# Attention and MLP on one core: five value buffers, later query transfers, a later LayerNorm subtraction, and turns of seven heads at the end

## The chip, the cores and the metric

The kernel runs on one NeuronCore of a Trainium2 chip. TensorE (PE in the profile; PEld are its weight loads) multiplies, ScalarE (ACT) does exponentials, GELU and copies, VectorE (DVE) does maxima, subtractions and the last scaling, GpSimd (POOL) does element-wise work in on-chip memory, and SyncE (SP) issues transfers. ScalarE and GpSimd issue transfers too. Products land in PSUM, eight banks of 128 x 512 float32. The metric is the device time of one execution in microseconds (us); three runs of the kernel before are shown.

## The reference

```python
g = sigmoid((x * gate_w).sum(-1, keepdims=True))
a = attention(x, wqkv, wo)      # 16 heads of 28, no mask, softmax over 2048 keys
b = gelu(layernorm(x) @ w1 + b1) @ w2 + b2
return g * a + (1 - g) * b      # x: (1, 2048, 448), all float32; MLP width 1792
```

LayerNorm has no weights (eps 1e-5), GELU is the tanh form.

## The kernel before

Every float32 operand is split into a high part that the fast float32 product takes exactly and a low rest; a product is high x high + high x low + low x high. A contraction runs over 32 rows at a time: the 128 rows of the array make four *strips*, and four instructions on different strips run side by side.

**First stage: a planner.** The class `Strips` writes the order of the TensorE instructions by simulating the four strips with costs and due times of its own. Its pieces of work are `QK` (queries and keys), `Val` (values and the gate's sum), `Up` and `Down` (the two MLP products), each over one bank of banks 0 to 5, each visited by all four strips in some order. When one strip is done with a piece and the next may add to the same bank, SyncE passes the word on (line 529, `hand`; three times for each of 113 pieces, 339 in all): so a transfer that SyncE has to issue, or has to wait for, stands in the same queue as these hand-offs. `st.at(t, fn)` puts `fn` into the program where the planner's clock reaches `t`; the engines keep that order.

Between the pieces the planner puts *row maxima* (`RowMax`): a product of 128 queries with 512 keys into bank 6 or 7 (line 212), and VectorE's maximum of it (line 214). There are 1024, counted by strip and by chunk n (four heads x 512 queries, 16 chunks); softmax needs them before the exponentials. When a strip has ended chunk n, the queries of chunk n + 2 are fetched into the same half of `qd` (`load_q`, line 196), set by line 511 at the planner's time plus 1.5.

`Val.close` (line 322) has ScalarE copy a finished bank into `vt[i % 3]` and send it to memory (`vs<-vt`, line 328). LayerNorm of x goes by chunks c of 512 tokens (`want_ln`): x is loaded, the mean subtracted (VectorE for c of 0 and 1, line 683; GpSimd after that, line 679), multiplied by 1/std (line 688), split into `yh` (ScalarE, line 704) and `yl` (GpSimd, line 705), which `Up` reads.

**Second stage: turns.** The attention proper has 1024 *heads* (a strip's key block of 128 against 512 queries). `turn_of` takes five or six of them: two halves of at most three. For each half PE makes three passes (line 1152: high x high, low x high, high x low), each head on its strip and in its bank, then ScalarE takes the exponentials of the half's banks in one instruction (line 1156) into `p0` or `p1`, three buffers each. `turn_bank` puts head i of a turn in bank (i + shift) % 6, shift being 0 or 3 as the first stage ended. Row maxima still owed are put between the passes (`lone`), in bank 6 or a free one: three in a turn of five, two in a turn of six. A turn has five heads only while more is owed than the turns up to the last 116 heads could take.

After a turn's scores come value products (`batch`, line 1164: four heads at once, into bank 7), of earlier turns' exponentials. In a turn of six `quota` allows one and a half batches, or two if more than two are behind; in other turns all that are there. When a chunk's 16 batches are done, `valued` has VectorE copy bank 7 into `ob`, fetch the sums, and GpSimd multiply (`finish_a`, `finish_b`, `finish_c`; the last chunk's `finish_last` does this and the projection in one go). In the last group of heads four *projections* follow, in turns 6 to 9 after the chunk (`tail`, `project`, lines 1001 to 1009: twelve products into bank 6, the weighted sum, the output).

Pool `ao` gives two buffers each to `ob`, `rc` and `lt` and six to `acc`; the raw output weights (`fetch_wo`) use `ob`.

Of the kernel before, what the change touches and what calls it, by code (L numbers as in the profile page):

```python
# [15 lines left out]
P = 128  # L16
S = 2048
D = 448
# [17 lines left out]
def kernel(ctx: ExitStack, tc: tile.TileContext, xt, wqk, wv, wo, xk, w1, b1, w2, b2,  # L36
# [84 lines left out]
    mr = px.tile([P, 2, NT], F32, name="mr")  # L121
    mrt = px.tile([P, 2 * NT], F32, name="mrt")
    std = px.tile([P, NT], F32, name="std")
    vt = [px.tile([P, H, 32], F32, name=f"vt{i}") for i in range(3)]

    bxr = [px.tile([P, 2, D], F32, name=f"bxr{i}") for i in range(2)]

# [173 lines left out]
    class Val(Piece):  # L301
# [18 lines left out]
            return ops  # L320

        def close(self, st, now):
            v, ps, tt = vt[self.i % 3], bk[:, self.bank], self.i
            nc.scalar.activation(v[:, :, 0:DH], ps[:, :D].rearrange("p (h d) -> p h d", d=DH), AF.Copy)
            nc.scalar.activation(zall[:, tt:tt + 1], ps[:, D:D + 1], AF.Copy)
            st.use("act", now + 0.2, 0.75)
            st.free[self.bank] = st.act + 0.1
            st.at(st.act + 0.3, lambda: nc.scalar.dma_start(vs[tt], v.rearrange("p (g j) d -> p g (j d)", g=NG)), act=0.35)
# [75 lines left out]
    class Strips:  # L404
# [92 lines left out]
        def rowmax(self, s, now):  # L497
            if now < self.hot[s] or not rowmax.ready(s):
                return False
            if rowmax.cnt[s] > 5 + min(rowmax.cnt):  # L500
                return False
            b = min(self.rm, key=lambda b: self.rm[b])
            if self.rm[b] > now:
                return False
            ends = rowmax.one(s, bk[:, b])
            self.t[s] = now + 0.232
            self.use("dve", now + 0.45, RM)
            self.rm[b] = self.dve + 0.1
            for kind, n, j in ends:
                if kind == "q":  # L510
                    self.at(now + 1.5, lambda n=n, j=j: rowmax.load_q(n, j))
                elif kind == "k":
                    def load(n=n, j=j):
                        rowmax.load_k(n, j)
                        self.hot[j] = self.get(self.clock + 0.6, 224) + 1.0

                    self.at(now + 1.5, load)
                    self.hot[j] = 1e9
                else:
                    self.at(now + 0.5, lambda n=n: rowmax.close(n), dve=0.45)  # L520
                    self.at(now + 3.0, lambda n=n: rowmax.store(n))
            return True
# [151 lines left out]
    def want_ln(st, c):  # L674
        cs = slice(c * CH, (c + 1) * CH)

        def use(t, r):
            if c > 1:
                nc.gpsimd.tensor_sub(r, r, lnr[c][:, 0])
                st.use("pool", st.clock, 1.35)  # L680
                scale(t, r)
                return
            nc.vector.tensor_sub(r, r, lnr[c][:, 0])
# [13 lines left out]
        st.feed.pump()  # L697
# [267 lines left out]
    wraw = {}  # L965

    def fetch_wo(g):
        wraw[g] = ao.tile([P, D], F32, name="ob")
        nc.sync.dma_start(wraw[g], wo[:, g])

    def split_wo(g):
# [45 lines left out]
    obs = {}  # L1017

    def finish_a(n):
        ob = ao.tile([P, CH], F32, name="ob")  # L1020
        lt = ao.tile([P, CH // 32], F32, name="lt")
        obs[n] = ob, lt
        nc.vector.tensor_copy(ob, pv)  # L1023
# [1 line left out]

    def finish_b(n):
        ob, lt = obs[n]
        rc = ao.tile([P, CH], F32, name="rc")
        obs[n] = ob, rc
        nc.vector.reciprocal(lt, lt)  # L1030
        r = rls[n]
# [13 lines left out]
    def finish_last(n):  # L1045

        g, c = divmod(n, NC)
        ob = ao.tile([P, CH], F32, name="ob")
        rc = ao.tile([P, CH], F32, name="rc")
# [78 lines left out]
    def turn_of(u, turn):  # L1128

        left = UNITS - u  # L1130
        owed = rowmax.left()
        size = min(left, 5 if owed and owed > 2 * ((left - 116) // 6) else 6)
        na, nb = min(3, size), max(0, size - 3)
        for x in range(u, u + size):
            n = x // 64
            if n not in begins:
                begins.add(n)
                begun(n, turn)
        extra = {5: ((0, 3, 6), (3, 1, 5), (5, 2, 6)), 6: ((0, 3, 6), (5, 2, 6))}.get(size, ())
        for half, first, count in ((0, 0, na), (1, 3, nb)):  # L1140
            for p in range(3):
                for x, o, b in extra:
                    if x == 3 * half + p:
# [1 line left out]
                for i in range(first, first + count):  # L1145
# [6 lines left out]
                    nc.tensor.matmul(bk[:, turn_bank(i)], w[r, ks], q[r], start=(p == 0), stop=(p == 2), skip_group_check=True)  # L1152
            if count:
                t = ap.tile([P, 3, CH], F32, name=f"p{half}")
                b = turn_bank(first)
                nc.scalar.activation(t[:, :count], bk[:, b:b + count], AF.Exp, scale=SCALE)  # L1156
                for i in range(count):
                    prob[u + first + i] = t[:, i]
# [14 lines left out]
    while b < UNITS // 4:  # L1173
        before, quota = u, 99
        if u < UNITS:
            u += turn_of(u, turn)
            if u - before == 6:
                quota = 3 + (before // 4 - b > 2)
        for fn in agenda.pop(turn, ()):
            fn()  # L1180
# [72 lines left out]
```

## Time and profile before

| what | value |
| --- | --- |
| runs | 1093.5, 1094.56, 1097.05 us; median 1094.56 |
| the profiled execution | 1093.69 us, its span 1091.9 us |
| mean granted TensorE clock | 0.996 |
| PE busy / PEld busy | 1074.4 us (98%) / 728.4 us (67%) |
| DVE / ACT / POOL busy | 740.4 / 634.0 / 368.7 us |
| row maxima before 455 us / after | 566 / 458 |
| last row maximum's product | 984.6 us |
| instructions | 30966 |

The first stage ends at about 455 us, when the first score products (line 1152) run. PE's busy time says little by itself: up to four strips overlap, and the record counts a moment as busy if any of them works. A wait shows as PE idle time only when all four strips have run dry. The waits name what came last; the chain that ended last tells where such a wait lay on the way to the end. All times are in us from the span's start unless they are marked ns.

### The profile page before, as it was taken

What the parts mean: (1) busy time and instruction counts of PE and PEld (TensorE: products, weight loads), DVE (VectorE), ACT (ScalarE), POOL (GpSimd) and SP (SyncE); (2) the same over time, 40 slices, a digit from 0 to 9 for tenths busy, and PEclk for the clock granted to TensorE, in tenths of its full rate; (3) what the DMA queues carried; (4) which work ended last, traced back from release to release, by engine and by line L of the source; (5) the groups of instructions that cost most, each with busy time, mean ns of one, the idle gap of its engine ahead of it and who ended that gap; (6) DMA issues with size and microseconds to landing.
All of it is one profiled execution on the core that took longest, in us unless ns stands there. A gap on an engine that the chain in (4) does not pass through costs nothing.

```text
span 1091.9 us, 30966 instructions
## 1 busy us (share of the span) xinstructions
PE 1074.4 (98%) x13394; PEld 728.4 (67%) x13394; DVE 740.4 (68%) x1186; ACT 634.0 (58%) x660; POOL 368.7 (34%) x384
## 2 busy tenths in 40 slices
PE   9999999999999999999999999999999999999998
PEld 7999998999899899844444444444444444454655
DVE  4899898898999999866776665667676544311102
ACT  5343363033043132287788788788787888857572
POOL 4565587336234037341001101310110313445431
PEclk9999999999999999999999999999999999999999
DMA  7696433212100104320000001300000201011111
GB/s 248 201 293 196 153 110 93 78 43 71 45 2 11 45 3 126 93 74 16 29 6 23 23 21 48 88 28 8 21 25 19 80 21 55 20 57 38 61 53 60
DMA packets 47785, 73.20 MB, mean 67 GB/s; under 512 B 13840, under 2 KB 28816, under 8 KB 46848
## 3 DMA queue, kind: packets, MB, share of 16 engines
q1 hardware_dynamic: 33888, 39.11, 11.8%
q0 software_dynamic: 5120, 16.89, 5.3%
q10 hardware_dynamic: 8640, 15.21, 3.9%
q8 instruction: 105, 1.72, 0.6%
q14 instruction: 32, 0.26, 0.1%
HBM read 51.75 MB, written 19.31 MB: 65 GB/s over the span
## 4 chain that ended last, share of the span: by engine, by line
PE 95%; ACT 1%; DMA 1%; DVE 1%; issue 1%; SPq 0%; DVEq 0%; ACTq 0%
PE bk L488 34%; PE bk L1164 22%; PE bk L1152 19%; PE bk L212 15%; PE bk L1001 1%; PE bk L1002 1%; PE bk L1003 1%; ACT p L1156 1%; PE bk L917 1%; DMA vs<-vt 1%; DMA gbs<-gb 1%; PE bk L902 0%; DVE ob L1023 0%; PE bk L945 0%; DVE acc L1008 0%
## 5 line engine op out<-in xcount | busy, mean ns | idle before, releaser
L214 DVE TENSOR_REDUCE mx<-bk 128x1 f32<-128x512 f32 x1024 | 674.2, 688 | 219.5 <-PE bk L212 188.4
L1156 ACT ACTIVATE p<-bk 128x1536 f32<-128x1536 f32 (+1 forms) x387 | 481.8, 1298 | 135.4 <-PE bk L1152 129.4
L212 PE MATMUL bk<-kd,qd 28*128 28x512 f32 x1024 | 449.2, 441 | 2.8 <-DVE acc L1008 1.7
L212 PEld LDWEIGHTS bk<-kd,qd 28*128 28x128 f32 x1024 | 186.4, 182 | 186.6 <-DVE mx L214 117.2
L488 PE MATMUL bk<-yh,w1f 32*128 32x512 f32 x1568 | 188.6, 393 | 2.5 <-ACT gb L398 2.5
L488 PE MATMUL bk<-yl,w1f 32*128 32x512 f32 x784 | 164.2, 393 | 0.0
L488 PEld LDWEIGHTS bk<-yh,w1f 32*128 32x128 f32 x1568 | 151.1, 183 | 5.7 <-ACT gb L398 3.7
L488 PE MATMUL bk<-w2h,hh 32*128 32x448 f32 x896 | 140.6, 368 | 2.2 <-SPq L529 2.2
L488 PE MATMUL bk<-w2l,hh 32*128 32x448 f32 x896 | 140.0, 366 | 0.0
L1164 PE MATMUL bk<-p,va 128*32 128x512 f32 (+1 forms) x1080 | 130.6, 579 | 0.0
L1164 PE MATMUL bk<-p,vb 128*32 128x512 f32 (+1 forms) x1192 | 129.4, 540 | 0.0
L363 POOL TENSOR_TENSOR hl<-h,hh 128x512 fp32r<-128x512 f32 x56 | 72.3, 1301 | 140.5 <-ACT hh L356 79.3
L837 POOL CAST yh<-yl 128x512 fp32r<-128x512 f32 x16 | 9.8, 614 | 285.7 <-PE bk L212 89.7
L1152 PE MATMUL bk<-yh,ka 29*128 29x512 f32 x512 | 104.3, 481 | 0.6 <-ACT p L1156 0.6
L488 PEld LDWEIGHTS bk<-w2h,hh 32*128 32x128 f32 x896 | 102.2, 185 | 3.3 <-SPq L529 2.6
L488 PEld LDWEIGHTS bk<-yl,w1f 32*128 32x128 f32 x784 | 103.3, 184 | 0.3
L488 PEld LDWEIGHTS bk<-w2l,hh 32*128 32x128 f32 x896 | 102.3, 185 | 0.1
L1152 PE MATMUL bk<-yh,kb 29*128 29x512 f32 x512 | 96.8, 478 | 0.7 <-ACT p L1156 0.5
L398 ACT ACTIVATE gb<-bk 128x448 f32<-128x448 f32 x14 | 7.6, 545 | 140.1 <-PE bk L488 98.8
L488 PE MATMUL bk<-w2h,hl 32*128 32x448 f32 x896 | 88.0, 362 | 0.0
L1152 PE MATMUL bk<-yh,la 28*128 28x512 f32 x512 | 86.3, 392 | 0.0
L1152 PE MATMUL bk<-yl,ka 28*128 28x512 f32 x512 | 84.7, 410 | 0.0
(141 smaller groups left out, 1603.5 us busy)
## 6 DMA issues: line engine op xcount, KB each, us to landing
qk<-qo ACTq DMA_DIRECT2D x28, 256.0 KB
raw<-in_xt SPq DMA_DIRECT2D x17, 256.0 KB
vs<-vt ACTq DMA_DIRECT2D x16, 256.0 KB
rc<-rls SPq DMA_DIRECT2D x60, 64.0 KB
bxr<-in_xk POOLq DMA_DIRECT2D x8, 448.0 KB, 6.1
acc<-gbs SPq DMA_DIRECT2D x16, 224.0 KB
out_y<-acc SPq DMA_DIRECT2D x16, 224.0 KB
qd<-qk SPq DMA_DIRECT2D x60, 56.0 KB
```

The costliest lines, as they stand in the source:

```text
L212: nc.tensor.matmul(ps, self.qd[n % 2][r, i * P:(i + 1) * P], self.kd[r, k * 512:(k + 1) * 512], start=True, stop=True)
L214: nc.vector.reduce_max(self.mx[n % 2][:, j, i, k:k + 1], ps, axis=AX)
L363: nc.gpsimd.tensor_sub(hl[f], h, hh[f].bitcast(F32))
L488: mm = nc.tensor.matmul(bk[:, x.bank, :n], a, b, start=x.first, stop=(len(x.rem) == 1 and m == len(ops) - 1), skip_group_check=True)
L837: nc.gpsimd.tensor_copy(h, l.bitcast(F32))
L917: nc.tensor.matmul(bk[:, b], w, v, start=(i == 0), stop=(i == len(ops) - 1), skip_group_check=True)
L1001: nc.tensor.matmul(po, h, woh[:, g], start=(g == 0), stop=False, skip_group_check=True)
L1002: nc.tensor.matmul(po, h, wol[:, g], start=False, stop=False, skip_group_check=True)
L1003: nc.tensor.matmul(po, l, woh[:, g], start=False, stop=(g == NG - 1), skip_group_check=True)
L1152: nc.tensor.matmul(bk[:, turn_bank(i)], w[r, ks], q[r], start=(p == 0), stop=(p == 2), skip_group_check=True)
L1156: nc.scalar.activation(t[:, :count], bk[:, b:b + count], AF.Exp, scale=SCALE)
L1164: nc.tensor.matmul(bk[32 * j:32 * j + 32, 7, sl], vg[n // NC][:, k, 32 * j:32 * j + 32], prob[4 * b + j][:, sl], start=(k == 0), stop=(k = ...
```

## The change

Five edits. `vt` has five buffers in place of three. `load_q` in the first stage is put at the planner's time plus 6.0 in place of 1.5. For chunk 0 of LayerNorm VectorE's subtraction is put 1.5 of the planner's time after its load is expected. The raw output weights use buffers of `acc`, and `ob` and `rc` have one buffer each. And a turn that begins with no row maximum owed takes seven heads, unless a projection is due in it or in the next turn: four heads in banks 0 to 3, three in banks 4 to 6; `p0` gets room for four.

```diff
-    vt = [px.tile([P, H, 32], F32, name=f"vt{i}") for i in range(3)]
+    vt = [px.tile([P, H, 32], F32, name=f"vt{i}") for i in range(5)]
...
-            v, ps, tt = vt[self.i % 3], bk[:, self.bank], self.i
+            v, ps, tt = vt[self.i % 5], bk[:, self.bank], self.i
...
-                    self.at(now + 1.5, lambda n=n, j=j: rowmax.load_q(n, j))
+                    self.at(now + 6.0, lambda n=n, j=j: rowmax.load_q(n, j))
...
-        def use(t, r):
+        def use(t, r, late=False):
             if c > 1:
                 nc.gpsimd.tensor_sub(r, r, lnr[c][:, 0])
                 st.use("pool", st.clock, 1.35)
                 scale(t, r)
+                return
+            if c == 0 and not late:
+                st.at(st.clock + 1.5, lambda: use(t, r, True))
                 return
             nc.vector.tensor_sub(r, r, lnr[c][:, 0])
...
-        wraw[g] = ao.tile([P, D], F32, name="ob")
+        wraw[g] = ao.tile([P, D], F32, name="acc", bufs=6)
...
-        ob = ao.tile([P, CH], F32, name="ob")
+        ob = ao.tile([P, CH], F32, name="ob", bufs=1)
...
-        rc = ao.tile([P, CH], F32, name="rc")
+        rc = ao.tile([P, CH], F32, name="rc", bufs=1)
...
-        size = min(left, 5 if owed and owed > 2 * ((left - 116) // 6) else 6)
-        na, nb = min(3, size), max(0, size - 3)
+        size = 5 if owed and owed > 2 * ((left - 116) // 6) else 6
+        if not owed and not (tail and tail[0][0] <= turn + 1):
+            size = 7
+        size = min(left, size)
+        na = min(4 if size == 7 else 3, size)
+        nb = size - na
...
-        for half, first, count in ((0, 0, na), (1, 3, nb)):
+        place = (lambda i: i) if size == 7 else turn_bank
+        for half, first, count in ((0, 0, na), (1, na, nb)):
...
-                    nc.tensor.matmul(bk[:, turn_bank(i)], w[r, ks], q[r], ...)
+                    nc.tensor.matmul(bk[:, place(i)], w[r, ks], q[r], ...)
             if count:
-                t = ap.tile([P, 3, CH], F32, name=f"p{half}")
-                b = turn_bank(first)
+                t = ap.tile([P, 4 - half, CH], F32, name=f"p{half}")
+                b = place(first)
...
-            if u - before == 6:
+            if u - before > 5:
                 quota = 3 + (before // 4 - b > 2)
```

More of the change, by code (lines that the diff above doesn't have):

```diff
@@ L1047, in finish_last @@
         g, c = divmod(n, NC)
-        ob = ao.tile([P, CH], F32, name="ob")
-        rc = ao.tile([P, CH], F32, name="rc")
+        ob = ao.tile([P, CH], F32, name="ob", bufs=1)
+        rc = ao.tile([P, CH], F32, name="rc", bufs=1)
         lt = ao.tile([P, CH // 32], F32, name="lt")
@@ L1151, in turn_of @@
                     q = (qh, qh, ql)[p][n % 3]
-                    nc.tensor.matmul(bk[:, turn_bank(i)], w[r, ks], q[r], start=(p == 0), stop=(p == 2), skip_group_check=True)
+                    nc.tensor.matmul(bk[:, place(i)], w[r, ks], q[r], start=(p == 0), stop=(p == 2), skip_group_check=True)
             if count:
-                t = ap.tile([P, 3, CH], F32, name=f"p{half}")
-                b = turn_bank(first)
+                t = ap.tile([P, 4 - half, CH], F32, name=f"p{half}")
+                b = place(first)
                 nc.scalar.activation(t[:, :count], bk[:, b:b + count], AF.Exp, scale=SCALE)
```

## The prediction

> **What bounds the kernel now.** I read the page first, its busy times and the chain that ended last.
>
> ```profile
> PE 1074.4 (98%) x13394; PEld 728.4 (67%) x13394; DVE 740.4 (68%) x1186; ACT 634.0 (58%) x660; POOL 368.7 (34%) x384
> PE 95%; ACT 1%; DMA 1%; DVE 1%; issue 1%; SPq 0%; DVEq 0%; ACTq 0%
> ```
>
> TensorE carries 95% of the chain, so an edit pays only where it shortens PE's own work or takes away a moment in which all strips stand still. Such moments are few. I looked for them in the list of waits, then in the chain around 100 us, then in busy times by short stretches (columns: stretch, length, PE, PEld, DVE, ACT, POOL busy, granted clock, DMA share, GB/s).
>
> ```profile
> PE bk L488 <- SPq L529: 2.2, 1, 2.2
> PE bk L488 <- ACT zall L325: 1.9, 1, 1.9
> ACT vt L324 <- DMA vs<-vt: 8.8, 2, 6.8
> ```
> ```profile
> 101.41 7.29 DMA vs<-vt
> 109.43 0.47 PE bk L488
> ```
> ```profile
> 110.00:114.00 4.00, 4.00 (x52) 4.00 (x50) 3.31 (x6) 0.00 (x0) 1.27 (x1) 0.60 0.37 139
> 192.00:196.00 4.00, 4.00 (x52) 3.96 (x56) 2.12 (x4) 0.00 (x0) 1.24 (x1) 0.61 0.78 257
> 296.00:300.00 4.00, 2.96 (x49) 2.67 (x52) 2.66 (x5) 1.09 (x2) 0.00 (x0) 1.00 0.44 162
> ```
>
> The two longest stops of PE in the first stage are 1.9 us (behind ScalarE, itself 6.8 us behind a value transfer) and 2.2 us (behind a hand-off on SyncE). After each the granted clock is 0.60 over four us, so 4 x 0.4 = 1.6 us of work are lost on top. The stop of 1.0 us at 296 (PE busy 2.96 of 4.00) left it at 1.00. The changed turns lie behind 985 us.
>
> **The change part by part.**
>
> *Five value buffers.*
>
> ```profile
> 92.41 0.33 ACTq L328 DMA_DIRECT2D vs<-vt  x1
> 98.40 0.33 ACTq L328 DMA_DIRECT2D vs<-vt  x1
> 100.04 0.55 ACT L324 ACTIVATE vt<-bk 128x448 f32<-128x448 f32 x1 [1.61 <-PE bk L488]
> 108.77 0.54 ACT L324 ACTIVATE vt<-bk 128x448 f32<-128x448 f32 x1 [6.83 <-DMA vs<-vt]
> ```
>
> The sixth copy waits for the third buffer, sent at 98.40 and landed at 108.7. With five buffers it takes the first, sent at 92.41 and free by 100.04, where the fourth copy waited for PE alone. The third buffer is then wanted two pieces later, after 108.7. The wait goes, and with it 1.9 us of stop and 1.6 us of slow clock: -3.5 us. Bounds: -3.5, and 0 if something else is late at that place (a rival).
>
> ```profile
> L874 POOL MEMSET vt<- 128x48 f32 x3 | 0.4, 139 | 0.0
> ```
>
> Four more small memsets on GpSimd at the start stand ahead of any data: nothing; uncovered, four of at most 139 ns would cost 0.6 us.
>
> The Trainium skill ("TensorE: Matmul & The Clock Gate", section "Why this matters for your kernels") says that idle gaps of PE up to about 3 us do not throttle it. By that rule the buffers would be worth 1.9 us alone and the sum below would be -1.5 us. The trace disagrees: a stop of 1.9 us was followed by a clock of 0.60.
>
> *Later query transfers.* SyncE's queue around the other stop:
>
> ```profile
> 184.56 0.34 SPq L196 DMA_DIRECT2D qd<-qk  x1
> 187.96 2.58 SPq L569 DMA_DIRECT2D raw<-in_xt  x4
> 190.65 0.98 SPq L196 DMA_DIRECT2D qd<-qk  x1
> ```
>
> Four loads of 2.58 us and one query load stand between two hand-offs; PE waits for the second. Moved by 4.5 us, the load at 190.65 leaves this place, but the one at 184.56 comes to 189.1, into the same burst. So I take 0. Bounds: -2.6 us (the 0.98 us of its issue, and the 1.6 us of clock, since a stop of 1.0 keeps it), and +1.0 us, one load more in the burst. The queries themselves are not late: their next use is a whole chunk, 64 maxima, later. Behind a waiting `load_q` on SyncE stand hand-offs, and PE behind these; key loads now pass the query loads, which are four short issues.
>
> *Later subtraction.* VectorE is the in-order engine here; row maxima queue behind it, and through banks 6 and 7 PE.
>
> ```profile
> L571 POOL DMA_DIRECT2D raw<-in_xt x4: 539/539/557, 100.2 to 101.8; - x4
> DMA to landing us min/median/max: 6.8/8.0/9.5
> ```
> ```profile
> 110.59 0.68 DVE L683 TENSOR_TENSOR raw<-raw,lnr 128x512 f32<-128x512 f32 x1
> 124.75 1.29 POOL L705 TENSOR_TENSOR yl<-raw,yh 128x512 fp32r<-128x512 f32 x1 [1.26 <-ACT yh L704]
> 126.86 0.49 PE L488 MATMUL bk<-yh,w1f 32*128 32x512 f32 x2
> ```
>
> The four loads land between 107 and 111. The first subtraction ran at 110.59, held up by the very stop that goes; 3.5 us earlier it would stand at 107.1 and wait for its load. At 1.5 us later it stands at 108.6, behind the first landing. It cannot gain against the kernel before, where no idle time stands ahead of line 683; it keeps the first edit's gain: 0, and as the upper bound the first rival below.
>
> *Buffers of the second stage.* `ob` and `rc` single: the copy of chunk n waits for GpSimd's use of chunk n - 1, set four turns after that chunk, and a chunk is nine turns or more. Five turns of 3 us cover it: 0. Without cover bank 7 would be held. The weights in `acc` take SyncE's waits for two `ob` buffers away; nobody on the path waited for them: 0.
>
> *Turns of seven.* From ScalarE's rows behind 985 us (duration min/median/max; and start, duration of a run of instructions):
>
> ```profile
> L1156 ACT ACTIVATE p<-bk x43: 1024/1451/1468, 985.8 to 1072.5; 128x1536 f32<-128x1536 f32 x42, 128x1024 f32<-128x1024 f32 x1
> ```
> ```profile
> 985.79 2.79 ACT L1156 ACTIVATE p<-bk 128x1536 f32<-128x1536 f32 x2 [3.92 <-PE bk L1152]
> 988.78 5.48 ACT L1156 ACTIVATE p<-bk 128x1536 f32<-128x1536 f32 x4 [0.20 <-PE bk L1152]
> 1005.20 2.79 ACT L1156 ACTIVATE p<-bk 128x1536 f32<-128x1536 f32 x2 [0.24 <-PE bk L1152]
> 1072.51 1.02 ACT L1156 ACTIVATE p<-bk 128x1024 f32<-128x1024 f32 x1 [2.87 <-PE bk L1152]
> ```
>
> 42 x 3 + 2 = 128 heads, six of them in the turn at 985.79, which holds the last row maximum: 122 heads remain. Before, these are 20 turns of six and one of two; eight carry a projection. Following the new rule by hand (chunk 13 ends in the first of them, chunk 14 ten turns later): five turns of seven, five of six, five of seven, three of six, one of four. That is two turns fewer; the last projection of chunk 14 falls behind the last chunk's own.
>
> What a turn costs, from the chain:
>
> ```profile
> 999.29 1.86 PE bk L1164 x24
> 1001.15 1.60 PE bk L1152 x13
> 1002.75 1.43 PE bk L1164 x16
> 1004.18 1.80 PE bk L1152 x13
> 1061.77 1.43 PE bk L1164 x16
> 1065.83 1.59 PE bk L1152 x16
> ```
> ```profile
> 1004.11 0.19 PEld L1152 LDWEIGHTS bk<-yh,kb 29*128 29x128 f32 x3 [0.84 <-ACT p L1156]
> 1005.01 0.19 PEld L1152 LDWEIGHTS bk<-yh,kb 29*128 29x128 f32 x3 [0.36 <-ACT p L1156]
> ```
>
> Scores take 1.60 us, values 1.43 for one and a half batches and 1.86 for two (0.86 a batch and 0.14), a projection 1065.83 - 1061.77 - 1.43 = 2.63. Seven heads are six passes as six are, the fourth strip being free: 1.60 too. The turn at 1004.11 took 1.80, since its second half began at 1005.01, when the exponentials of the previous second half had ended (1002.16 + 2.79 = 4.95 less 1000): 0.20 late.
>
> Without waits: two turns less 2 x (1.60 + 0.14) = -3.5, the last turn of four in place of two +0.4, one projection less ahead of the end -2.6: -5.7. Behind the end the late projection adds:
>
> ```profile
> 1086.57 0.22 PE bk L1003
> 1087.94 0.59 DVE acc L1008
> ```
>
> PE is free at 1086.8; twelve products at about 0.21 (the row of the last one is 0.22) end by 1089.4, and VectorE's 0.59 behind them at 1090.1, where now it ends at 1088.5: +1.6.
>
> ```profile
> L1156 ACT ACTIVATE p<-bk 128x1536 f32<-128x1536 f32 x250 | 356.3, 1451 | 132.5 <-PE bk L1152 126.5 <-PE bk L212 5.9
> L1156 ACT ACTIVATE p<-bk 128x1024 f32<-128x1024 f32 x137 | 139.6, 1019 | 2.9 <-PE bk L1152 2.9
> ```
>
> The waits grow. A four-bank exponential is not in the trace; 1019 ns for two banks and 1451 for three give 1.88 for four. With 1.45 for the second and 0.11 of overlap (5.48 for four of 1.45) a turn's exponentials end 1.09 + 3.22 = 4.31 after its scores began, against 3.88 now. I carried this row by row through the turns: each half starts when its strip is free and its banks' exponentials ended 0.06 ago. For the kernel before it gives 83.8 us from 988.78 to 1072.51, measured 83.7, of them 2.1 us of waits. For the sevens it gives 6.6: besides the second halves there is a change of banks at each change of kind. Into the first seven, banks 0 to 3 hold the previous second half's (0.9); out of a seven into a six whose first half has banks 3 to 5, it waits again (0.5 and 1.35). By the plan of the kernel before the sixes start at bank 3; started at 0 the waits are 5.4. So +4.5, or +3.3.
>
> Tail: -5.7 + 1.6 + 4.5 = +0.4 us, with the other bank order -0.8; bounds -4.1 (no new waits) and +7.3 (a rival).
>
> **Sum.** -3.5 + 0 + 0 + 0.4 = -3.1 on the profiled execution's 1093.69: 1090.6. The runs' median is 0.9 above that execution; I take half of that on top, 1091.0. A run or two of this kernel can tell about 0.3%, 3.3 us; the forecast lies at that edge.
>
> **The rivals.**
>
> *The gain is handed back by LayerNorm.* `yl` ended at 126.04 and PE began `Up` at 126.86. PE comes 3.5 us sooner; if the late subtraction keeps the chain of loads, VectorE and GpSimd where it was, PE stops 2.7 us there and the clock falls again (1.6). Against it: the chain now also loses ScalarE's second wait for a value buffer (the rest of the 8.8). Then 1091.0 + 4.3 = 1095.3.
>
> *More goes than I count.* The stop at 189 shrinks (-2.6), and the bank order is the better one (-1.2): 1091 - 3.8 = 1087.2. For it: both follow the new plan, whose order I cannot see.
>
> *ScalarE holds every seven.* If a seven's first scores wait for the whole previous turn, it takes 4.38 us in place of 3.69 on the average of my rows: ten times, 6.9 us, 1097.9. It makes the change slower by over 0.3% (1097.8) from 0.68 us a turn on. Against it: the turn at 1004.11 began while exponentials ran to 1004.95. The Trainium skill ("TensorEngine Tiling (Array Packing)", section "PSUM Bottleneck") warns that packing the array does not speed up the emptying of PSUM, which may become the bound. The trace agrees in so far as ScalarE's 3.1 us a seven is close to PE's 3.46 (1.60 + 1.86).
>
> *The new plan stops PE elsewhere.* A hand-off behind a burst as at 189 costs 2.2 + 1.6 = 3.8: 1094.8 for one; two, at 1098.6, make the change slower. For it: every time in the plan behind 100 us moves. Against it: the trace has one such stop among the 339 hand-offs.
>
> **How the numbers follow.** My case 0.38, its own range 1088.5 to 1093; handed back 0.20; more goes 0.20; ScalarE holds 0.10; stops elsewhere 0.12. Faster by over 0.3% (below 1091.3): 0.20 and 0.23 of my case, 0.43. Slower (above 1097.8): the third and under half of the last, 0.15. The rest, 0.42, is within. The range 1086 to 1097 leaves out the third, half of the last, and a little below.
>
> **What would show it.** Right: no wait of ScalarE for `vs<-vt`, the clock at 1.00 from 110 to 114, the first scores 3 to 4 us sooner; exponentials of 2048 in ten rows at 1.88; sevens between 3.0 and 4.4 us; the last projection behind the last chunk's; from the first turn with nothing owed to the end within 1.5 us of the 103 us now. Wrong: a stop of PE near 125 or in another burst of SyncE, sevens all at 4.4 us or all at 3.2.

## The result, and the profile after

The changed kernel took 1086.29 us (median of six runs) beside 1094.51 us for the kernel before: a ratio of 0.9921, 95% interval 0.9898 to 0.9944. Timed a second time it took 1086.96 beside 1093.12, ratio 0.9943 (0.9924 to 0.9962). So 6 to 8 us went, where 3.5 were forecast. The profiled execution took 1087.38 us, its span is 1085.6 us. Most runs of a kernel lie within some 3 us of its median, single ones up to 8 us off, and one execution of e1, of 4896.37 us, is not in its ratio. Short stops of TensorE in the first stage that cost more in one execution than in another are a part of this (last section); differences of medians under 1.5 us are not read as anything below.

The profile page after, busy times and the chain that ended last:

```profile
PE 1068.0 (98%) x13450; PEld 724.0 (67%) x13450; DVE 740.1 (68%) x1186; ACT 633.3 (58%) x652; POOL 367.7 (34%) x388
PE 94%; ACT 2%; DMA 1%; issue 1%; DVE 1%; SPq 0%; DVEq 0%; ACTq 0%
```

Nothing in these two lines tells the kernels apart: PE is busy 98% of the span in both. The stretches around the two old stops do (columns as in the prediction), and so does the list of PE's waits (total, times, longest):

```profile
110.00:114.00 4.00, 4.00 (x77) 3.97 (x76) 3.56 (x6) 1.74 (x5) 1.81 (x2) 1.00 0.42 156
192.00:196.00 4.00, 3.16 (x61) 2.75 (x54) 3.70 (x6) 0.00 (x0) 2.16 (x2) 1.00 0.36 113
296.00:300.00 4.00, 4.00 (x73) 3.76 (x70) 4.00 (x7) 2.64 (x4) 1.65 (x2) 1.00 0.15 57
```
```profile
PE bk L488 <- issue: 1.9, 2, 0.9
PE bk L488 <- ACT gb L398: 1.4, 2, 1.1
```

The waits of 1.9 us for `zall` and of 2.2 us for a hand-off on SyncE are gone, no other wait of PE in that list is longer than 1.6 us, and the clock is 1.00 in each of the three stretches.

Where did the time go? The exponentials of line 1156 (line 1164 after) begin when the second stage begins, and the answer for one line gives their first and last start (before, then after):

```profile
L1156 ACT ACTIVATE p<-bk x387: 1015/1451/1471, 456.9 to 1072.5; 128x1536 f32<-128x1536 f32 x193, 128x1024 f32<-128x1024 f32 x1
```
```profile
L1164 ACT ACTIVATE p<-bk x379: 597/1450/1885, 453.7 to 1062.7; 128x1536 f32<-128x1536 f32 x179, 128x2048 f32<-128x2048 f32 x10, 128x512 f32<-128x512 f32 x1
```

The first stage got 3.2 us shorter (456.9 to 453.7) and the second 3.1 us (1091.9 - 456.9 = 635.0 to 1085.6 - 453.7 = 631.9). The forecast had the whole gain in the first stage and a small loss in the second. 578 row maxima lie before the first scores in place of 566.

### The profile page after: what moved, and what is told of

It reads as the page before. It is cut to its first block, busy times and chain, and to the rows that moved or that the text cites. A ratio compares the mean times of both kernels' runs of the same rounds, so it can differ in the third digit from the quotient of the medians.

```text
span 1085.6 us, 31067 instructions
## 1 busy us (share of the span) xinstructions
PE 1068.0 (98%) x13450; PEld 724.0 (67%) x13450; DVE 740.1 (68%) x1186; ACT 633.3 (58%) x652; POOL 367.7 (34%) x388
## 3 DMA queue, kind: packets, MB, share of 16 engines
q8 instruction: 105, 1.72, 0.7%
## 4 chain that ended last, share of the span: by engine, by line
PE 94%; ACT 2%; DMA 1%; issue 1%; DVE 1%; SPq 0%; DVEq 0%; ACTq 0%
PE bk L488 35%; PE bk L1172 21%; PE bk L1160 18%; PE bk L212 15%; ACT p L1164 2%; PE bk L1004 1%; PE bk L1006 1%; PE bk L1005 1%; PE bk L920 1%; DMA gbs<-gb 1%; DMA first<-in_xt 0%; DVE acc L1011 0%; DMA kd<-qk 0%; DVE ob L1026 0%; PE bk L948 0%
## 5 line engine op out<-in xcount | busy, mean ns | idle before, releaser
L1164 ACT ACTIVATE p<-bk 128x1536 f32<-128x1536 f32 (+2 forms) x379 | 480.8, 1322 | 129.6 <-PE bk L1160 128.0
L488 PE MATMUL bk<-yh,w1f 32*128 32x512 f32 x1568 | 192.7, 393 | 1.4 <-ACT gb L398 1.4
L488 PE MATMUL bk<-yl,w1f 32*128 32x512 f32 x784 | 167.2, 391 | 0.0
L488 PEld LDWEIGHTS bk<-yh,w1f 32*128 32x128 f32 x1568 | 154.0, 183 | 4.1 <-ACT gb L398 2.5
L488 PE MATMUL bk<-w2h,hh 32*128 32x448 f32 x896 | 145.4, 366 | 0.9 <-issue 0.9
L488 PE MATMUL bk<-w2l,hh 32*128 32x448 f32 x896 | 144.4, 364 | 0.0
L1160 PE MATMUL bk<-yh,ka 29*128 29x512 f32 x512 | 101.5, 483 | 0.6 <-ACT p L1164 0.6
L488 PE MATMUL bk<-w2h,hl 32*128 32x448 f32 x896 | 93.4, 363 | 0.0
L1160 PE MATMUL bk<-yh,la 28*128 28x512 f32 x512 | 83.6, 392 | 0.0
```

Source lines behind the costliest of these rows:

```text
L488: mm = nc.tensor.matmul(bk[:, x.bank, :n], a, b, start=x.first, stop=(len(x.rem) == 1 and m == len(ops) - 1), skip_group_check=True)
L1160: nc.tensor.matmul(bk[:, place(i)], w[r, ks], q[r], start=(p == 0), stop=(p == 2), skip_group_check=True)
```

## The experiments

Each run below gives its median, that of the kernel before beside it, and the ratio with its interval. "First stage" is the time of the first exponential in the profiled execution, "second" the rest of its span. The kernel before was timed anew beside each group of runs, so runs of different groups are compared by their ratios.

| run | us | before | ratio (95%) | first | second | maxima in first |
| --- | --- | --- | --- | --- | --- | --- |
| kernel before (e16: again) | | | | 456.9 (456.8) | 635.0 (635.0) | 566 |
| e1 value buffers alone | 1089.93 | 1093.82 | 0.9962 (0.9937-0.9986) | 455.1 | 633.3 | 566 |
| e2 later queries alone | 1089.79 | 1093.82 | 0.9965 (0.9944-0.9986) | 456.1 | 633.3 | 566 |
| e3 later subtraction alone | 1089.63 | 1093.82 | 0.9961 (0.9939-0.9983) | 459.4 | 632.9 | 578 |
| e4 sevens, `ao` buffers alone | 1095.88 | 1093.82 | 1.0018 (0.9998-1.0037) | 454.9 | 635.7 | 566 |
| e5 change without sevens | 1086.80 | 1093.12 | 0.9940 (0.9921-0.9959) | 454.6 | 631.1 | 578 |
| e10 change again | 1086.96 | 1093.12 | 0.9943 (0.9924-0.9962) | 454.0 | 632.2 | 578 |
| e7 change, other banks | 1086.80 | 1093.12 | 0.9942 (0.9924-0.9961) | 453.7 | 631.8 | 578 |
| e9 before, limit 4 | 1087.45 | 1093.12 | 0.9949 (0.9929-0.9969) | 455.7 | 631.0 | 573 |
| e6 change without later subtraction | 1089.65 | 1093.83 | 0.9970 (0.9947-0.9993) | 448.7 | 636.0 | 566 |
| e11 before, maxima capped | 1096.64 | 1093.83 | 1.0020 (0.9997-1.0043) | 453.7 | 638.4 | 552 |
| e12 same with later subtraction | 1094.71 | 1093.83 | 1.0009 (0.9991-1.0027) | 452.3 | 638.3 | 552 |
| e13 e1 + e2 + limit 4 | 1088.70 | 1093.83 | 0.9954 (0.9938-0.9971) | 453.6 | 631.4 | 573 |
| e14 queries on GpSimd | 1087.05 | 1094.59 | 0.9934 (0.9914-0.9954) | 450.8 | 633.0 | 566 |
| e15 e5, queries on GpSimd | 1089.81 | 1094.59 | 0.9957 (0.9941-0.9973) | 455.3 | 632.7 | 578 |
| e8 later subtraction, 1.2 | 1081.30 | 1094.59 | 0.9885 (0.9854-0.9916) | 447.2 | 631.3 | 570 |
| e17 e8 + e1 | 1080.97 | 1092.95 | 0.9890 (0.9868-0.9913) | 446.5 | 632.6 | 570 |
| e18 change with 1.2 | 1078.43 | 1092.95 | 0.9863 (0.9841-0.9884) | 445.9 | 630.8 | 570 |

The profiled execution of e3 was the slowest of its ten, those of e6 and e13 the fastest of their own, which their first stages show.

### The four parts alone: e1, e2, e3, e4

Each is the kernel before with one part of the diff shown above (the main lines of three here; e4 has the rest). The theory on trial was the prediction's sum.

```diff
-    vt = [px.tile([P, H, 32], F32, name=f"vt{i}") for i in range(3)]      # e1
+    vt = [px.tile([P, H, 32], F32, name=f"vt{i}") for i in range(5)]
...
-                    self.at(now + 1.5, lambda n=n, j=j: rowmax.load_q(n, j))   # e2
+                    self.at(now + 6.0, lambda n=n, j=j: rowmax.load_q(n, j))
...
+            if c == 0 and not late:                                       # e3
+                st.at(st.clock + 1.5, lambda: use(t, r, True))
+                return
```

> The kernel before with five value buffers alone. The prediction: the 1.9 us stop near 108 and the 1.6 us of slow clock behind it go, -3.5 us, and the first score product comes 3.5 us sooner (452.4 in place of 455.9); the order of TensorE's instructions is unchanged, 136 turns of five. The rival reading of the two traces: this edit alone leaves VectorE's first LayerNorm subtraction waiting for its load, part of the stop stays, and the gain is 1 to 2 us.

> The kernel before with the later query transfers alone. The prediction: 0, between -2.6 and +1.0 us, the stop of PE near 190 stays at about 2.2 us because another query load moves into the burst. The rival, from the trace of the changed kernel, where the clock near 192 stays at 1.00: this edit takes the load out of the burst, the stop shrinks to about 1 us, the clock stays up, -2.6 us.

> The kernel before with the later LayerNorm subtraction alone. The prediction: 0. The rival: the edit makes the planner place 578 row maxima in the first stage in place of 566, and the slowest strip has 143 in place of 138; 452 are owed in place of 472, 122 turns of five in place of 136, three turns fewer in all. At 2.96 us a turn of five and 3.23 a turn of six (from the two traces) that is -14 x 2.96 + 12 x 3.23 = -2.7 us in all, against which the first stage keeps both long stops.

> The kernel before with the turns of seven and the buffers of the second stage alone: nothing of the first stage changes. The prediction: +0.4 us, 103.5 us from the first turn with nothing owed to the end (103.1 before), with 6.6 us of waits in the turns of seven and the last projection behind the last chunk's. The rival: the sevens save about one turn of six, 2 to 4 us, since the waits for banks are hidden.

By the medians the buffers brought 3.9 us, where 3.5 were forecast. The query transfers, forecast at 0, brought 4.0; the later subtraction, forecast at 0, brought 4.2. The sevens cost 2.1 (interval -0.2 to +4.0).

The traces show that not all of such a gain is the edit's. The second stage of e1, of e2 and of e14 below is 1.7 to 2.1 us shorter than that of the kernel before, although their edits leave it alone. ScalarE's waits go with this (the kernel before, then e1):

```profile
ACT p L1156 <- PE bk L1152: 129.4, 184, 3.9
ACT p L1156 <- PE bk L212: 5.9, 4, 1.5
```
```profile
ACT p L1156 <- PE bk L1152: 133.8, 189, 3.9
```

In both traces of the kernel before, four exponentials wait for a row maximum's product (line 212); in e1, e2 and e14 none does. Among kernels with one plan and the same turns, those with such waits have the longer second stage every time (566 maxima: 635.0 against 633.0 to 633.3; 578: 632.7 to 632.9 against 631.1; 573: 631.4 against 631.0; 570: 632.6 against 631.3). What brings these waits about no run shows.

In the first stage, kernels with one plan do the same row maxima in the same order, so the nth of one trace can be set against the nth of another. Between 103 and 125 us, where the value buffer's stop lies, e1 gains 2.5 us on the kernel before. But e2 and e4, with three buffers, gain 1.9 us there too, most of it because the clock did not drop behind their stop. So the price of that stop depends on the execution: the part for the clock is in it only where the clock drops.

The second stop: PE's first product behind it in the kernel before, then SyncE's queue, PE's product and the stretch in e2.

```profile
191.74 0.73 PE L488 MATMUL bk<-w2h,hh 32*128 32x448 f32 x1 [2.22 <-SPq L529]
```
```profile
187.44 2.34 SPq L569 DMA_DIRECT2D raw<-in_xt  x4
191.32 1.80 SPq L196 DMA_DIRECT2D qd<-qk  x3
```
```profile
189.90 0.46 PE L488 MATMUL bk<-w2h,hh 32*128 32x448 f32 x1 [0.90 <-SPq L529]
```
```profile
192.00:196.00 4.00, 4.00 (x85) 3.96 (x81) 3.92 (x7) 0.00 (x0) 2.20 (x2) 1.00 0.75 245
```

Before, a query load was issued 3.4 us ahead of the burst and one right behind it (at 190.65, for 0.98 us), and PE went on at 191.74, when that one was through. In e2 the queries come at 191.32, and PE goes on at 189.90, right behind the burst's end at 187.44 + 2.34 = 189.78. The stop is 0.9 us in place of 2.2, and the clock stays at 1.00 where it was 0.61: 1.3 + 1.6 of the 4.0 us are seen at this place. The maxima say the same: between 185 and 196 us e2 gains 2.9 us on the kernel before.

In e4 PE's wait for exponentials heads its list, 4.5 us against 1.2 before, and one wait is there that the kernel before does not have and I had not listed: twelve products into bank 6 wait until VectorE has emptied it of the projection ahead of them. It is not the sevens' own, since e5, e11 and e13 have it too.

```profile
PE bk L1157 <- ACT p L1161: 4.5, 9, 0.9
PE bk L1001 <- DVE acc L1008: 0.8, 1, 0.8
```

### The change without its sevens, and with other banks: e5, e7, e10

> The changed kernel without the turns of seven (sixes throughout once nothing is owed; all other edits kept). The prediction priced the sevens at +0.4 us and the run of the sevens alone at 1.0018: then this kernel is 0.4 to 2 us faster than the changed one, with 69 turns of six and 23 us less of... no projection left behind the last chunk. The rival: the sevens pay where fewer maxima are owed, and this kernel is 1 to 3 us slower than the changed one.

> The changed kernel with the turns of seven in banks that follow the turns of six: the first four heads in banks 3 to 6 and the last three in 0 to 2 (the sixes start at bank 3). The prediction's reckoning of the waits: the three changes of banks (0.9 + 0.5 + 1.35 us) go, -2.7 us against the changed kernel; ScalarE's idle time ahead of the first seven falls from about 1.1 to 0.2. The rival: these waits only move to the second half of the turn, and nothing changes.

> The changed kernel once more, beside the two below on the same chip. All theories: 0.992 of the kernel before, as measured first.

e5 drops the rule for sevens. e7 keeps it, with the second stage's shift of 3 taken into account:

```diff
-        na = min(4 if size == 7 else 3, size)
+        na = min(4 if size == 7 and shift else 3, size)      # e7: banks 3 to 6, then 0 to 2
...
-        place = (lambda i: i) if size == 7 else turn_bank
+        place = (lambda i: (i + shift) % 7) if size == 7 else turn_bank
```

All three are at 1086.8 to 1087.0: the sevens are worth nothing that can be told beside the mends (the other edits of the change). ScalarE's rows show why the other banks gained nothing either: the wait moved. After, the change of kind out of the sevens into a six has ScalarE idle 1.12 us (997.95), into the first seven 2.99 us; in e7 the way out costs 0.78 and the way in 3.85 (after, then e7).

```profile
979.78 6.46 ACT L1164 ACTIVATE p<-bk 128x2048 f32<-128x2048 f32 x4 [2.99 <-PE bk L1160]
986.47 3.22 ACT L1164 ACTIVATE p<-bk 128x2048 f32<-128x2048 f32 x2 [0.24 <-PE bk L1160]
990.14 3.22 ACT L1164 ACTIVATE p<-bk 128x2048 f32<-128x2048 f32 x2 [0.44 <-PE bk L1160]
993.61 3.22 ACT L1164 ACTIVATE p<-bk 128x2048 f32<-128x2048 f32 x2 [0.25 <-PE bk L1160]
997.95 2.79 ACT L1164 ACTIVATE p<-bk 128x1536 f32<-128x1536 f32 x2 [1.12 <-PE bk L1160]
```
```profile
980.50 6.33 ACT L1164 ACTIVATE p<-bk 128x2048 f32<-128x2048 f32 x4 [3.85 <-PE bk L1160]
994.32 5.91 ACT L1164 ACTIVATE p<-bk 128x2048 f32<-128x2048 f32 x4 [0.37 <-PE bk L1160]
1001.01 2.79 ACT L1164 ACTIVATE p<-bk 128x1536 f32<-128x1536 f32 x2 [0.78 <-PE bk L1160]
```

### What the later subtraction does: e9, e6, e11, e12

My second theory was "turns": the late subtraction makes the planner write another order, in which twelve more maxima are done in the first stage, so fewer turns of five are left. e9 reaches a like count by another edit, with none of the change in it:

```diff
-            if rowmax.cnt[s] > 5 + min(rowmax.cnt):
+            if rowmax.cnt[s] > 4 + min(rowmax.cnt):
```

> The kernel before with one number of the planner changed: a strip may be 4 row maxima ahead of the slowest in place of 5. No edit of the change is in it. The planner then places 573 maxima in the first stage (566 before), the slowest strip has 142 (138), 456 are owed (472), and 125 turns have five heads (136). If the gain of the later subtraction comes from the plan (fewer owed, fewer turns of five), this kernel's attention from the first to the last score product is 3 to 4 us shorter than before and the whole 2 to 3 us faster. If that gain comes from VectorE's not waiting near 109 us, it is 0.

> The changed kernel without the late subtraction: the order of the kernel before (566 maxima, 472 owed), five value buffers, later query transfers, turns of seven. If the edits add up: 1093.8 - 3.9 - 4.0 + 2.0 = 1087.9 by the medians of the single edits. If the late subtraction is worth its 4.2 us beside the others too: 1090.5 to 1091.

e9 gained 5.7 us from a 5 made a 4, nearly as much as the whole change. Its second stage is 2.0 to 4.0 us shorter than those of the kernels with 566 maxima and old turns (633.0 to 635.0). But that is not all of it: its first stage has no stop at 110 us either, without a single value buffer more.

```profile
108.00:112.00 4.00, 4.00 (x79) 3.93 (x78) 4.00 (x8) 0.00 (x0) 1.23 (x1) 1.00 0.97 375
```

e11 and e12 hold the number of maxima fixed, at 138 for each strip, without and with the late subtraction:

```diff
-            if rowmax.cnt[s] > 5 + min(rowmax.cnt):
+            if rowmax.cnt[s] >= 138 or rowmax.cnt[s] > 5 + min(rowmax.cnt):
```

> Kernel before with at most 138 row maxima per strip in the first stage, so 552 there in place of 566; the smallest strip has 138 in both, so 472 are owed in both and the turns are the same but for one (137 turns of five and 56 of six in place of 136 and 57). It serves as the base of the next run. Both theories: within 1.5 us of the kernel before (14 products fewer are 14 x 0.23 / 4 = 0.8 us of the strips, one turn of five more about +0.5).

> The late subtraction alone with the same cap of 138: first stage re-planned, second stage the same turns as in the run with the cap alone. Theory 'turns' (the late subtraction's 4.2 us come from fewer maxima owed and so fewer turns of five): within 1 us of the cap alone. Theory 'first stage' (they come from an order of the first stage with fewer or shorter stops of PE): 2.5 to 4 us less than the cap alone, and the first scores 2 to 4 us sooner.

With equal counts the second stages are equal (638.4 and 638.3), so the late subtraction acts there only through the count. In the medians e12 is 1.9 us ahead of e11, between what either theory gave and not clear of the noise, and 1.4 us in the profiled first stages. The cap prices a maximum, too: 14 more in the second stage made it 3.4 us longer than in the kernel before (638.4 against 635.0, both with the four waits for a row maximum), and 12 fewer made it 1.9 to 2.2 us shorter in e5 than in e1, e2 and e14 (none with such waits): about 0.2 us each. I had expected the cap to change nothing, since the number owed by the smallest strip is the same; that was wrong, every maximum left over is worked off. By that price the twelve more maxima are worth 2 to 3 us of the second stage, some half of the 4.2.

The rest is another order of the first stage, and the traces show what is better in it: e3 and e12 have no stop behind a hand-off at 190 us, though their query transfers come at the old time; e11 has one of 1.9 us. Both keep a stop behind the value buffer (4.4 and 1.7 us, last section). e6 agrees with the part of the count: without the late subtraction the change loses 3.0 us (1089.65 against 1086.6 or so), and its second stage is 4.1 us longer than after, of which some 1.7 us go with the four waits for a row maximum, which e6 has and after has not.

### Do the gains add: e13

> Kernel before with five value buffers, the later query transfers and a limit of 4 in place of 5, neither the late subtraction nor turns of seven. The order is that of the run with the limit of 4 alone (573 maxima in the first stage, 456 owed), whose one long stop was 1.8 us behind a hand-off. If the later query transfers take that stop away as they did at 189 us: 1084.0 to 1085.5, some 1.5 us below the changed kernel. If the gains are one and the same (an order without the stop at 110 us): as the limit alone, 1087.5 beside a kernel before of 1093.1.

The diffs of e1, e2 and e9 together were no better than e9 alone. A stop of 1.7 us behind a hand-off stayed, which the later transfers did not touch in this order: there the four loads alone stand ahead of it. Nor do the parts of the change add: e1, e2, e3 and e4 sum to -10.0 us, the change itself is at -6.2 to -8.2. The intervals of the parts are wide enough for that, but two reasons can be seen. e2 and e3 both take away the stop at 190 us, and the shorter second stage of e1 and e2 can come only once. In the changed kernel, then, the later transfers may have had little left to do; no run drops them alone.

### SyncE's queue alone: e14, e15, e16

The forecast for the query transfers had failed by more than its bounds, so I changed their queue and not their time:

```diff
-                    self.at(now + 1.5, lambda n=n, j=j: rowmax.load_q(n, j))
+                    self.at(now + 1.5, lambda n=n, j=j: rowmax.load_q(n, j, nc.gpsimd))
```

> Kernel before with the query transfers of the first stage issued on GpSimd in place of SyncE, at the old time (plus 1.5). The order of the first stage is that of the kernel before. Theory 'SyncE's queue' (the stop of 2.2 us at 190 us came from the query transfer that stood between two hand-offs): 1089.5 to 1091, the stop there 1 us or less and the clock at 1.00, as with the later transfers. Rival (the burst of four x loads alone makes the stop, the later transfers won elsewhere): within 1 us of the kernel before. A cost on the other side: GpSimd's queue waits where the half of qd is not yet free, which would show as idle time of GpSimd ahead of the query transfers.

> The changed kernel without turns of seven, and the query transfers on GpSimd at plus 1.5 in place of SyncE at plus 6.0. If SyncE's queue is all that counts: 1086 to 1087.5, as with the later time. If the transfers wanted the later time for another reason: 1089 to 1091.

> The kernel before once more, for a second trace. The order is fixed, so the two long stops (behind the value buffer at 109 us and behind the hand-off at 190 us) should stand there again, with the granted clock below 0.9 in the 4 us behind at least one of them; first score to end 634 to 636.5 us.

```profile
185.55 2.42 SPq L569 DMA_DIRECT2D raw<-in_xt  x4
```
```profile
PE bk L488 <- SPq L529: 1.0, 1, 1.0
```
```profile
192.00:196.00 4.00, 4.00 (x86) 3.90 (x83) 3.86 (x9) 0.00 (x0) 2.39 (x2) 1.00 0.45 155
```

With the query loads off SyncE (its queue in e14 holds the burst alone) the stop is 1.0 us and the clock 1.00, as in e2: it is shown that the query load made the stop 2.2 us in place of 1.0. The 1.0 stays behind the four loads, so the rival is right by half. In the kernel before the stop stood again in the second trace, 2.2 us, as did the one for the value buffer, both with the clock below 0.7 behind them. e14 gained 7.5 us, more than this stop. Its profiled execution is 8.1 us shorter than that of the kernel before: 2.8 us of it are gained at the stop (185 to 196 us), 1.7 between 103 and 125 us, where the clock did not drop, and 2.1 in the second stage; the last two the edit does not touch. e15, the same edit beside the other mends, was 1.9 us behind e5 by the ratios. It has a new stop of 1.6 us behind VectorE, and the clock dropped behind it.

### Another lateness: e8, e17, e18

Would 1.2 of the planner's time do what 1.5 does? The load is waited for nearly as long, but the order written is another, with 570 maxima.

```diff
-                st.at(st.clock + 1.5, lambda: use(t, r, True))
+                st.at(st.clock + 1.2, lambda: use(t, r, True))
```

> The late subtraction alone, 1.2 of the planner's time late in place of 1.5. The plan then has 570 maxima in the first stage in place of 578, the smallest strip 139 in place of 143 (135 turns of five, 58 of six, one of one). From the first score to the end by the price of a maximum in the second stage (0.3 us): 4 fewer there than in the kernel before, 634.9 - 1.2 = 633.7 us. If the number of maxima carries half of the gain: 1091 to 1092.5. If the gain is that VectorE no longer waits for a load: as with 1.5, 1089.5.

> Late subtraction at 1.2 and five value buffers, nothing else. The order is that of the run with 1.2 alone, whose only long stop left in the first stage was 1.5 us behind a value buffer. Theory 'plan plus stops': that stop goes, 1079 to 1080.5. If the plan's order alone counts: 1081.3 as without the buffers. If the mends add up by their medians: 1081.3 - 3.9 = 1077.4.

> The changed kernel with its LayerNorm lateness at 1.2 in place of 1.5; the plan's first stage ends 5.1 earlier (422.6 in place of 427.7 of the planner's clock) with 570 maxima in place of 578. Theory 'plan plus stops': neither plan keeps a stop of over 1 us beside these mends, so the first stage ends 5 us sooner, the second (turns of seven, 8 maxima more in it) is 1 to 3 us longer: 1082 to 1084. If the mends add up on the lateness of 1.2: 1075 to 1078.

e8 is 13.3 us faster than the kernel before by this edit alone; e18, the changed kernel with one number different, is 14.5 us faster (1078.43, ratio 0.9863) and the fastest here. Neither of my theories for e8 came near. The first stage is 447.2 us, and few stops had been left to take away. A good part of the answer lies in the products of line 488 done in a stretch in which PE counts as busy nearly all the time. First line 488 alone, then all lines: the kernel before, after and e8, and of e18 line 488 alone, each from 200 to 400 us.

```profile
200.00:400.00 200.00, 197.49 (x3128) 186.48 (x3124) 1.00 0.10 34
200.00:400.00 200.00, 197.49 (x3416) 187.44 (x3412) 189.90 (x298) 56.09 (x90) 70.03 (x57) 1.00 0.10 34
```
```profile
200.00:400.00 200.00, 198.53 (x3112) 187.81 (x3109) 1.00 0.11 34
200.00:400.00 200.00, 198.57 (x3410) 188.69 (x3406) 195.26 (x306) 56.50 (x91) 69.85 (x56) 1.00 0.11 34
```
```profile
200.00:400.00 200.00, 199.38 (x3186) 189.87 (x3181) 1.00 0.11 34
200.00:400.00 200.00, 199.48 (x3485) 190.49 (x3480) 195.97 (x307) 59.16 (x96) 72.92 (x58) 1.00 0.11 34
```
```profile
200.00:400.00 200.00, 199.85 (x3190) 189.90 (x3187) 1.00 0.11 35
```

From after to e8 PE's busy time grows by 0.9 us of 200, its products by 75 (2.2%, 4.4 us of this stretch, where the first stages differ by 6.5) and those of line 488 by 74. A product lasts as long in both (0.38 us on the average). VectorE does as many maxima. The clock is 1.00 in all. The four strips overlap more of the time in the better order; "busy" can't show it, since one strip at work counts as much as four. The Trainium skill ("Perfetto Trace Analysis", section "Identifying the Most-Contended Engine") says that TensorE's matmul busy share is a poor measure of how far it is from its limit, and names two better ones, the arithmetic done as a share of the peak and the busy share of weight loads. The trace agrees on the first, which goes by the products done (2.2%), and in part on the second: weight loads grow by 1.0% where busy time grows by 0.5%.

In e17 the value buffers add nothing on that order that can be told (ratios 0.9890 and 0.9885), though they do take its stop of 1.5 us away; its second stage is longer by 1.3 us, and four exponentials in it wait for a row maximum. Why 1.2 packs the strips better than 1.5 I can't say: the order changes as a whole, and no run isolates one piece of it. But the planner's own clock had given the sign before the run (its first stage ends 5.1 sooner with 1.2, as expected for e18 above); measured it was 7.8 us (453.7 to 445.9).

## Why the prediction was wrong

The forecast was 1091.0 us within 1086 to 1097; the time lies at the lower edge of the range. By its own steps:

- **Five value buffers, -3.5: the wait was read rightly, the size came out with some luck.** After, PE is busy for the whole 4.00 us of the stretch from 110 us at a clock of 1.00. Alone the buffers gave -3.9 in the medians, but the first scores of e1's trace came 1.8 us sooner and not 3.5 (454.1 against 455.9), and its second stage gave the other 1.7. The term of 1.6 us for the clock holds only for executions in which the clock drops behind that stop; behind the same stop in e2, e4 and e14 it did not. One detail of what was to be seen was wrong, too: after, ScalarE still waits once, for 4.2 us at 110.88, for a buffer that is being sent; PE no longer stops long behind it.
- **Later query transfers, 0 with bounds -2.6 and +1.0: wrong, -4.0.** The step that failed is "the load at 184.56 comes to 189.1, into the same burst". I added the planner's 4.5 to a time of the trace. The planner's time sets an order, and SyncE runs that order: the load moved behind the burst and behind hand-offs, to 191.32 (e2). e14 shows that its place in SyncE's queue is what made the stop 2.2 us long. At this place 2.9 us were gained in e2 and 2.8 in e14, a little more than my bound of 2.6; the rest of the 4.0 is no more than e2's shorter second stage (1.7).
- **Later subtraction, 0: wrong, -4.2.** The failed step is "It cannot gain against the kernel before, where no idle time stands ahead of line 683". I looked for a wait to be removed. But the edit changes what the planner writes after it: 578 maxima in place of 566, at about 0.2 us each in the second stage (e11, e5), and a first stage without the stop at 190 us (e3, e12).
- **Buffers of the second stage, 0:** not seen apart from the sevens; in e4 no wait for `ob` or `rc` is among PE's waits.
- **Turns of seven, +0.4: right within what can be measured.** Beside the mends +0.2 (e10 against e5), alone +2.1 with an interval from -0.2 to +4.0; from the last row maximum's product to the end e4's trace takes 108.2 us, the kernel before's 107.3. Of its terms the four-bank exponential was 1.88 and measured 1879 ns (below); the turns of seven come every 3.34 to 3.67 us (979.78, 986.47 after two, 990.14, 993.61), inside 3.0 to 4.4; the wait out of the sevens is there at 997.95. The better bank order, which the second rival counted at 1.2 us, was not met as such; e7, which lets the sevens' banks follow those of the sixes, gained nothing.

```profile
L1164 ACT ACTIVATE p<-bk 128x2048 f32<-128x2048 f32 x10 | 18.8, 1879 | 7.8 <-PE bk L1160 7.8
```

Of the rivals, "more goes than I count" came nearest (1087.2), and half of its mechanism is real: the stop at 189 did shrink, in e2 by the later transfers and in e3 by the new order. "Handed back by LayerNorm" did not happen: after has no stop of PE between 120 and 180 us (60.00 us busy of 60.00). Nor did "ScalarE holds every seven" happen (the sevens come well under 4.4 us apart), nor "the new plan stops PE elsewhere": after has no long stop behind a hand-off. What no rival held is that the plan could get better as a whole. I had written "I cannot see" of its order, and let that stand for one old stop, a bank order or a new stop, when it should have widened both ends: e18 lies 6 to 9 us below the changed kernel, by three tenths of the planner's time.

## What to carry to other kernels

Where a program orders its own instructions by a cost model, an edit of one due time is an edit of the whole order: compare the new order with the old one (how much of each kind of work lies in which stage) before pricing single waits, and try neighbouring values, since 1.2 in place of 1.5 was worth as much here as the five edits together. Read a due time as a place in a queue, not as a time. Where TensorE counts as busy all the time, count its instructions in equal stretches. And set kernels that share an order against each other event by event: the gains of single edits held up to 2 us here that lay where the edit changes nothing.

## What the runs showed of the hardware that I had not expected

Whether the clock drops after a stop is not settled by the stop's length alone. In e12 and in e14 PE stopped once for 1.7 us behind the same value buffer, and in e3 for 4.4 us. The waits and the stretches, in that order (e3's second row is the stretch behind):

```profile
PE bk L488 <- ACT zall L325: 1.7, 1, 1.7
110.00:114.00 4.00, 4.00 (x55) 3.98 (x52) 2.85 (x5) 0.76 (x3) 0.78 (x1) 0.70 0.21 79
```
```profile
PE bk L488 <- ACT zall L325: 1.7, 1, 1.7
110.00:114.00 4.00, 4.00 (x79) 4.00 (x74) 4.00 (x8) 1.62 (x5) 2.68 (x2) 1.00 0.33 122
```
```profile
108.00:112.00 4.00, 0.00 (x0) 0.00 (x0) 0.32 (x1) 0.28 (x1) 0.00 (x0) 1.00 0.36 137
112.00:116.00 4.00, 3.62 (x40) 3.60 (x44) 1.80 (x3) 0.82 (x4) 0.00 (x0) 0.59 0.36 135
```

After 1.7 us the clock is 0.70 in one run and 1.00 in the other (55 and 79 products in 4 us); after 4.4 us it is 0.59, no lower than the 0.60 after 1.9 us in the kernel before.

What settles it is where the stop falls. In all 20 traces the granted clock changes only at whole multiples of 3.41 us behind the first change that the trace holds, and every drop ahead of the end of the run is one such stretch at 0.50: 1.7 us of work lost, whatever the stop's length. Cut at these moments, e12's stop lies whole in one stretch, which leaves PE 1.71 us of 3.41 busy, and the next stretch is at 0.50. e14's is split over two (2.62 and 2.48 busy), and nothing follows (e12, then e14):

```profile
105.55:108.96 3.41, 1.71 (x34) 1.18 (x30) 1.68 (x3) 1.00 (x4) 0.00 (x0) 1.00 0.76 285
108.96:112.37 3.41, 3.41 (x44) 3.41 (x40) 1.91 (x3) 0.10 (x2) 0.00 (x0) 0.50 0.45 168
```
```profile
104.43:107.84 3.41, 2.62 (x50) 2.06 (x43) 2.91 (x5) 0.00 (x0) 0.00 (x0) 1.00 0.97 348
107.84:111.25 3.41, 2.48 (x48) 2.47 (x51) 1.94 (x4) 1.11 (x4) 0.56 (x1) 1.00 0.62 235
```

Of all such stretches up to the last 16 us, each with 1.77 us or more idle was followed by a drop (ten of them) and none with 1.54 or less; between these, 1.64 and 1.70 were and 1.72 was not. So a stop of near 2 us costs its length and, if about half of one stretch falls to it, 1.7 us more. This may be a good part of why the runs of one kernel differ by some 3 us each way. The Trainium skill ("TensorE: Matmul & The Clock Gate", section "What's actually happening") tells of an activity window of some 3.4 us that runs on its own and does not start with the work, and of a drop after at least one idle window. The traces agree on the window; for the drop about half a window of idle time was enough here.
